# Loads and transforms dealt out as single operations, and in another order, between the steps of two matmul layers

## The chip, the cores and the metric

One Trainium2 chip, one of its cores. Device time in microseconds of one execution; several runs of each kernel, of which the median is given. TensorE, VectorE (DVE), ScalarE (ACT), GpSimd (POOL) and SyncE (SP) each work through a queue of their own, in order, and wait for each other by semaphores.

## What is computed

A two-dimensional Fourier transform of eight sequences of 3008 x 256, of which the real part goes through an MLP with 2048 hidden units.

```python
batch, seq, dim = (8, 3008, 256)
X = np.fft.fft(x, axis=1)
X = np.fft.fft(X, axis=2)
x = X.real.astype(np.float32).reshape(batch * seq, dim)
h = x @ w_in                       # 256 x 2048
r = np.maximum(h, 0.0)
g = s * (r * r) + b
out = (g @ w_out).astype(np.float32)   # 2048 x 256
```

## The kernel before

The transform along the features is folded into `w_in` at the start, and the symmetry of the real transform leaves 1506 columns of each sequence to be computed, each with two outputs ("pm" 0 and 1). The columns of a sequence are cut into three blocks of about 500 (some of 512), and each block goes through 16 steps, one for each 128 hidden units: 8 x 3 x 16 = 384 steps. Precision is kept by splitting each operand into a high part and a low rest and multiplying three times (high by high, low by high, high by low).

A step has these parts. The **first layer** (letter `L`, `first_layer`, L856): six matmuls of 500 columns into one of two pairs of PSUM banks, `ab`. Then the step's **group** on VectorE: L859, L860, L861 read `ab` and write `h`; with the third the banks are free for the first layer two steps later. ScalarE does L874, L875 (relu and square) and L876 (the high part `gh`), and GpSimd L880 the low part `gl` = `h` - `gh`. `h`, `gh` and `gl` have three buffers each. The **second layer** of a step (letter `S`, L897): twelve matmuls on `gh` and `gl` of a step two to four back, summed over the 16 steps of a block in four PSUM banks `po`; after the last, VectorE's L917 (four times) brings the sums out.

Between the steps the next sequences are prepared. `load` takes a sequence in eight tiles of 384 KB; for each a **front part** of three VectorE operations on the tile `xt` (L584, L585, L586), and a **back part** of two (L588, L589) that write `cs`, behind which the fetch of the tile two further on is issued on SP's queue (L575). `transform` (twice a sequence, `ph` 0 and 1) makes inputs (L433, L434, L442 to L446, L424), multiplies them by tables on TensorE (L684, into an `ab` bank pair that it holds until its sums are read), adds the results (L689, L690, L695) and stores them as the first layer's operands: high parts on ScalarE (L667), low ones on GpSimd (L670).

The order of all this is written out by hand. The string `START` deals out the first 57 steps, and `BATCH` is then gone through once for each 48 steps, a **round**: six full rounds with preparation, at about 293 to 1470 us, and one of 39 steps without. In `BATCH` the letter `L` means first layer, group, high and low part of one step, `S` the second layer of the oldest step that has none yet, `l` the next piece of `load`, `v` and `o` the next piece of the two transforms. A piece is what a generator does up to its next `yield`: before, a whole front part, a whole back part, all sums of one transform stage, and so on. At the end `_in_order` ties every engine's instructions to the order in which they were written. Steps are counted here from 1 to 48 within a round, so the 16 steps of a block end with steps 7, 23 and 39.

Of the kernel before, what the change touches and what calls it, by code (L numbers as in the profile page):

```python
# [67 lines left out]
BATCH = (  # L68
# [3 lines left out]
)  # L72
# [218 lines left out]
def kernel(ctx: ExitStack, tc: tile.TileContext, xq, xn, dft, turn, feat, w_in, w_out, s, b, out):  # L291
# [128 lines left out]
    def stt(dst, a, col, other, engine=nc.vector):  # L420
# [4 lines left out]
        else:  # L425
            engine.tensor_mul(dst, a, factor.broadcast_to(dst.shape))
            engine.tensor_add(dst, dst, other)

    def leaves_x(ph, cs, lf, engine=nc.vector):

        a, b_ = cs[:, 2], cs[:, 3]
        if ph == 0:
            engine.tensor_add(lf[:, 0], a, b_)  # L433
            engine.tensor_sub(lf[:, 1], a, b_)  # L434
        else:
            stt(lf[:, 0], b_, 0, a, engine)
            stt(lf[:, 1], a, 4, b_, engine)

    def leaves_y(ph, cs, uv, lf, engine=nc.vector):

        if ph == 0:
            engine.tensor_add(uv[:, :2], cs[:, 4:6], cs[:, 6:])  # L442
            engine.tensor_sub(uv[:, 2:], cs[:, 4:6], cs[:, 6:])
            yield
            engine.tensor_add(lf[:, 0], uv[:, 0], uv[:, 1])
            engine.tensor_sub(lf[:, 1], uv[:, 0], uv[:, 1])  # L446
            stt(lf[:, 2], uv[:, 3], 0, uv[:, 2], engine)
            stt(lf[:, 3], uv[:, 2], 4, uv[:, 3], engine)
        else:
            stt(uv[:, 0], cs[:, 6], 1, cs[:, 4], engine)  # L450
            stt(uv[:, 1], cs[:, 4], 5, cs[:, 6], engine)
            stt(uv[:, 2], cs[:, 7], 2, cs[:, 5], engine)
            stt(uv[:, 3], cs[:, 5], 6, cs[:, 7], engine)
            yield
            stt(lf[:, 0], uv[:, 2], 3, uv[:, 0], engine)
            stt(lf[:, 1], uv[:, 3], 7, uv[:, 1], engine)
            stt(lf[:, 2], uv[:, 2], 7, uv[:, 0], engine)
            stt(lf[:, 3], uv[:, 3], 3, uv[:, 1], engine)
        yield
# [8 lines left out]
    def nyquist(ph, t, room):  # L468
# [109 lines left out]
    def load(su):  # L578

        cs = fold.tile([P, 2, 8, 2 * P], F32, name="cs")  # L580
        folded[su] = cs
        for c in range(8):
            t = fetched.pop(0)
            add(t[:, 0::2], t[:, 0::2], t[:, 1::2])  # L584
            add(t[:, 1], t[:, 0], t[:, 2])  # L585
            sub(t[:, 3], t[:, 0], t[:, 2])  # L586
            yield
            add(cs[:R, :, c, :P], t[:, 1::2, :P], t[:, 1::2, P:])  # L588
            sub(cs[:R, :, c, P:], t[:, 1::2, :P], t[:, 1::2, P:])  # L589
            if 8 * su + c + 2 < 8 * NB:  # L590
                fetch(8 * su + c + 2)
            yield
# [79 lines left out]
    def transform(su, ph):  # L672
# [27 lines left out]

        lf = fold.tile([R, 4, 2 * P], F32, name="lf")
        leaves_x(ph, cs, lf[:, 2:])
        yield
        held, t, l = yield from pair(0, [cs[:, i] for i in range(2)])
        x0 = t[:, :, 2 * NL:].rearrange("p k (r a g) -> p k r a g", r=4, a=2)
        both(x0[:, :, :, 0], x0[:, :, :, 1], *map(by_residue, two(t, l)))
        banks.give(held)
# [3 lines left out]
        if ph == 0:  # L711
            x1 = l.rearrange("p k i (r g) -> p k (i r) g", r=2)
        else:
            x1 = t[:, :, 2 * NL:]
            both(x1[:, :, :NL], x1[:, :, NL:], *two(t, l))
            x1 = by_residue(x1)
        both(x[:, :, :, :2 * G], x[:, :, :, 2 * G:], x0, x1)
        banks.give(held)
# [3 lines left out]
        uv = small.tile([R, 4, 2 * P], F32, name="uv", tag="tmp")  # L722
        y_inputs = leaves_y(ph, cs, uv, lf)
        next(y_inputs)
        yield
        next(y_inputs)
        yield
        for i in range(2):
            held, t, l = yield from pair(4 + 2 * i, [lf[:, 2 * i + n] for n in range(2)])
            if ph == 0 and i == 0:  # L730
                y, which = l, slice(0, 2)
            else:
                y = t[:, :, 2 * NL:].rearrange("p k (r g) -> p k r g", r=2)
                both(y[:, :, 0], y[:, :, 1], *two(t, l))
                which = slice(i, 4, 2) if ph else slice(2, 4)
            o = fold.tile([P, 2, 2, 2, NL], F32, name="o")
            both(o[:, :, :, 0], o[:, :, :, 1], x[:, :, which], y)
            banks.give(held)
            o = o.rearrange("p k r a g -> p k r (a g)")
# [259 lines left out]

    def first():  # L1000
# [6 lines left out]
        steps.append(((su, blk, j), first_layer(su, blk, j, ebc[n])))  # L1007
# [44 lines left out]
    su = 1  # L1052
    while step < NB * NBLOCKS * NJ:
# [48 lines left out]
```

## Time and profile before

| | |
|---|---|
| median of 3 runs | 1677.92 us (1677.06 to 1678.57) |
| the profiled execution | 1679.25 us |
| its span, first to last instruction | 1677.3 us |
| granted TensorE clock, mean over the span | 0.999 |
| busy: PE, DVE, ACT, POOL | 1645.9, 1334.0, 1242.9, 975.6 us |
| bytes moved, mean rate | 67.44 MB, 40 GB/s |

The rows further down come from that one execution. A row of a timeline has the start in us from the span's start, the length in us, engine, line, operation, output<-input, shape, and in brackets the idle time of that engine just ahead of it and what ended it. A matmul's printed length is a model and longer than the distance to the next one. In a list of waits the three numbers are us in total, times, and the longest.

### The profile page before, as it was taken

The numbers are of one execution on the slowest core, as the hardware profiler recorded it, in microseconds if no ns is written. First come the engines' busy times: TensorE is split into PE (matmuls) and PEld (weight loads), VectorE is DVE, ScalarE is ACT, GpSimd is POOL, SyncE is SP. The second block draws the span as 40 slices with busy tenths as digits, with TensorE's granted clock in tenths as the row PEclk, the third lists the DMA queues.
The fourth block names the chain that finished last, engine by engine and source line by source line (L and its number), as shares of the span: only waits on it lengthen the run. The fifth ranks groups of instructions, "written<-read, shape, count | busy, mean of one in ns | idle before, by whom it ended". The sixth has DMA issues, their size and how long they took to land.

```text
span 1677.3 us, 21438 instructions
## 1 busy us (share of the span) xinstructions
PE 1645.9 (98%) x7592; PEld 1374.0 (82%) x7592; DVE 1334.0 (80%) x2010; ACT 1242.9 (74%) x1308; POOL 975.6 (58%) x542
## 2 busy tenths in 40 slices
PE   8999999999999999999999999999999999999998
PEld 5788788788887888878888788887888888888887
DVE  7999989996779867798677976879767896775554
ACT  4986666677686777867777777767878678787776
POOL 5664344555575556655656566555666556666565
PEclk9999999999999999999999999999999999999999
DMA  8211201120012100121100201102001110000100
GB/s 233 77 38 50 69 20 31 38 70 31 1 32 72 35 31 1 41 63 35 32 27 15 72 26 31 31 26 73 18 23 32 38 50 32 1 32 8 24 25 25
DMA packets 34320, 67.44 MB, mean 40 GB/s; under 512 B 7683, under 2 KB 24899, under 8 KB 34214
## 3 DMA queue, kind: packets, MB, share of 16 engines
q1 hardware_dynamic: 34214, 66.09, 13.2%
q8 instruction: 59, 0.97, 0.2%
q14 instruction: 47, 0.39, 0.1%
HBM read 41.35 MB, written 24.73 MB: 39 GB/s over the span
## 4 chain that ended last, share of the span: by engine, by line
PE 79%; DVE 14%; issue 3%; DMA 2%; ACT 1%; POOL 0%; POOLq 0%; SPq 0%; DVEq 0%; ACTq 0%
PE po L897 50%; PE ab L856 25%; PE ab L684 3%; DVE h L859 3%; DVE h L860 3%; DVE xt L584 2%; DVE h L861 2%; DVE xt L586 1%; DVE cs L589 1%; DVE cs L588 1%; DMA raw<-in_w_in 1%; DMA xt<-in_xq 1%; DVE xt L585 0%; ACT h L875 0%; ACT h L874 0%
## 5 line engine op out<-in xcount | busy, mean ns | idle before, releaser
L880 POOL TENSOR_TENSOR gl<-h,gh 128x1000 fp32r<-128x1000 f32 (+2 forms) x365 | 867.9, 2378 | 636.7 <-ACT gh L876 514.2
L874 ACT ACTIVATE h<-h 128x1000 f32<-128x1000 f32 (+2 forms) x380 | 395.3, 1040 | 351.2 <-DVE h L861 347.6
L859 DVE SCALAR_TENSOR_TENSOR h<-ebc,wny,ab 128x500 f32<-128x500 f32 (+1 forms) x384 | 280.8, 731 | 269.5 <-PE ab L856 150.5
L897 PE MATMUL po<-gh,wo_h 128*128 128x500 f32 (+2 forms) x1536 | 470.2, 387 | 0.0
L897 PE MATMUL po<-gl,wo_h 128*128 128x500 f32 (+2 forms) x1536 | 466.6, 385 | 0.8 <-POOL gl L880 0.8
L897 PE MATMUL po<-gh,wo_l 128*128 128x500 f32 (+2 forms) x1536 | 466.2, 385 | 0.0
L876 ACT CAST gh<-h 128x1000 fp32r<-128x1000 f32 (+2 forms) x385 | 397.4, 1032 | 35.2 <-PE po L897 15.8
L875 ACT ACTIVATE h<-h 128x1000 f32<-128x1000 f32 (+2 forms) x380 | 396.2, 1043 | 12.1
L897 PEld LDWEIGHTS po<-gl,wo_h 128*128 128x128 f32 x1536 | 288.1, 188 | 55.8 <-POOL gl L880 3.5
L897 PEld LDWEIGHTS po<-gh,wo_l 128*128 128x128 f32 x1536 | 288.6, 188 | 52.7
L897 PEld LDWEIGHTS po<-gh,wo_h 128*128 128x128 f32 x1536 | 285.8, 188 | 50.8
L856 PE MATMUL ab<-spec_h,wd_h 128*128 128x500 f32 (+1 forms) x768 | 301.5, 393 | 21.9 <-DVE h L861 21.0
L856 PE MATMUL ab<-spec_l,wd_h 128*128 128x500 f32 (+1 forms) x768 | 295.5, 385 | 0.2 <-DVE spec_l L670 0.2
L856 PE MATMUL ab<-spec_h,wd_l 128*128 128x500 f32 (+1 forms) x768 | 295.3, 385 | 0.0
L860 DVE TENSOR_TENSOR h<-h,ab 128x500 f32<-128x500 f32 (+1 forms) x384 | 260.0, 677 | 13.2
L861 DVE TENSOR_TENSOR h<-h,ab 128x500 f32<-128x500 f32 (+1 forms) x384 | 259.9, 677 | 13.2
L856 PEld LDWEIGHTS ab<-spec_h,wd_h 128*128 128x128 f32 x768 | 144.2, 188 | 62.0 <-DVE h L861 34.9
L856 PEld LDWEIGHTS ab<-spec_h,wd_l 128*128 128x128 f32 x768 | 144.3, 188 | 26.6
L856 PEld LDWEIGHTS ab<-spec_l,wd_h 128*128 128x128 f32 x768 | 144.4, 188 | 24.4 <-DVE spec_l L670 0.5
L917 DVE TENSOR_SCALAR o<-po,sb_s,bias 128x500 f32<-128x500 f32 (+1 forms) x94 | 68.8, 795 | 8.7 <-PE po L897 8.6
L584 DVE TENSOR_TENSOR xt<-xt 96x512 f32<-96x512 f32 x56 | 73.7, 1315 | 0.0
L670 POOL TENSOR_TENSOR spec_l<-o,spec_h 128x368 fp32r<-128x368 f32 (+7 forms) x75 | 60.0, 813 | 18.9 <-ACT spec_h L667 17.7
(128 smaller groups left out, 775.4 us busy)
## 6 DMA issues: line engine op xcount, KB each, us to landing
xt<-in_xq SPq DMA_DIRECT2D x64, 384.0 KB
out<-o SPq DMA_DIRECT2D x38, 500.0 KB
raw<-in_w_in SPq DMA_DIRECT2D x8, 512.0 KB
raw<-in_w_out SPq DMA_DIRECT2D x8, 512.0 KB
out<-o SPq DMA_DIRECT2D x8, 506.0 KB
ebc<-e_dram SPq DMA_DIRECT2D x12, 250.0 KB
ebc<-e_dram SPq DMA_DIRECT2D x4, 253.0 KB
out<-o SPq DMA_DIRECT2D x4, 250.0 KB
```

The costliest lines, as they stand in the source:

```text
L584: add(t[:, 0::2], t[:, 0::2], t[:, 1::2])
L670: low_engine.tensor_sub(lo, src, hi.bitcast(F32))
L856: nc.tensor.matmul(ps[:, kind], w[:, kind, fj], m[:, kind], start=i == 0, stop=i == 2)
L859: nc.vector.scalar_tensor_tensor(h[:, 0], ebc, wny[:, j:j + 1], ps[:, 0], op0=ALU.mult, op1=ALU.add)
L860: sub(h[:, 1], h[:, 0], ps[:, 1])
L861: add(h[:, 0], h[:, 0], ps[:, 1])
L874: nc.scalar.activation(h[:, pm], h[:, pm], AF.Relu)
L875: nc.scalar.activation(h[:, pm], h[:, pm], AF.Square)
L876: nc.scalar.copy(gh[:, pm, :width], h[:, pm])
L880: engine.tensor_sub(gl[:, pm, :width], h[:, pm], gh[:, pm, :width].bitcast(F32))
L897: nc.tensor.matmul(po[2 * pm + dh][:, :n], l[:, j, dh * P:(dh + 1) * P], r[:, pm, :n], start=start and first, stop=stop and last,)
L917: nc.vector.tensor_scalar(dst, src, *args, ALU.mult, ALU.add)
```

## The change

`load`, `transform` and their helpers yield `MORE` behind every single operation, and a plain `yield` where a piece ended before. `START` takes pieces whole as before, by the new function `whole`. `BATCH` takes one operation for each letter: 40 `l`, 28 `v` and 36 `o` in place of 16, 11 and 11, and its order is new. A step can also be written `H`: its low part on GpSimd is then done in two operations, one for each of the two outputs (`V`, on VectorE, does not occur in the table). `H` stands at steps 16, 39 and 48. Excerpt:

```diff
 BATCH = (
-    "L l S L L S l S L l l S L l l S l L S l L S L S l L l L S S L L S l l S L l S S L L l L l S L v l S L S S L L S "
+    "L l S l l L L l l S S l l l L l l l S l l L l l S l l l L S l l L S L S l L l l L S l l S L L S l l "
+    "l l l S L l l l S S L l l L l l l S H v v l S L S l S L L S L v S v v v L v v v v v S L v v v v L S "
...
+    def whole(pieces):
+
+        for more in pieces:
+            if more is not MORE:
+                return
...
     def load(su):
...
             add(t[:, 0::2], t[:, 0::2], t[:, 1::2])
+            yield MORE
             add(t[:, 1], t[:, 0], t[:, 2])
+            yield MORE
             sub(t[:, 3], t[:, 0], t[:, 2])
             yield
             add(cs[:R, :, c, :P], t[:, 1::2, :P], t[:, 1::2, P:])
+            yield MORE
             sub(cs[:R, :, c, P:], t[:, 1::2, :P], t[:, 1::2, P:])
...
         def both(dst_a, dst_b, a, b_):
             add(dst_a, a, b_)
+            yield MORE
             sub(dst_b, a, b_)
...
-    def first_layer(su, blk, j, ebc):
+    def first_layer(su, blk, j, ebc, low):
...
-        engine = nc.vector if step in LOWS_OF_STEPS_ON_VECTOR else nc.gpsimd
-        for pm in rows:
+        engine = nc.vector if step in LOWS_OF_STEPS_ON_VECTOR or low == "V" else nc.gpsimd
+        for pm in rows if low != "H" else (0, 1):
             engine.tensor_sub(gl[:, pm, :width], h[:, pm], gh[:, pm, :width].bitcast(F32))
...
+        elif what in "uvol":
+            whole(work[what])
...
         for what in BATCH.split():
-            if what == "L" and step < NB * NBLOCKS * NJ:
-                first()
-                go_on_first()
-                next(lows.pop(0))
+            if what in "LHV":
+                if step < NB * NBLOCKS * NJ:
+                    first(what)
+                    go_on_first()
+                    next(lows.pop(0))
```

What it moves: of the load, the front part of the second tile from step 4 to behind the back part at step 3, and of the third and fourth tile likewise by one place; the fifth tile's front part is cut, L584 at step 8 and the other two at step 9, and its back part stands at step 10; the last L589 goes from step 16 to step 17. One L424 of the second transform goes from step 37 to 36. A second layer goes ahead of the first layer of step 24, and one ahead of that of step 44. All else on TensorE, VectorE and ScalarE stands as before; the lines after L32 carry other numbers (L584 to L589 are L597 to L605, L859 to L861 are L880 to L882, L880 is L901).

VectorE's queue in the second round, from the back part of step 3 on, before (`xt` with a number is one tile, `h` with a number one step):

```order
L588 TENSOR_TENSOR cs_4174<-xt_2996 96x2x128
L589 TENSOR_TENSOR cs_4174<-xt_2996 96x2x128
L859 SCALAR_TENSOR_TENSOR h_4259<-ebc_3580,wny_94,ab_4252 128x500
L860 TENSOR_TENSOR h_4259<-h_4259,ab_4252 128x500
L861 TENSOR_TENSOR h_4259<-h_4259,ab_4252 128x500
L584 TENSOR_TENSOR xt_3055<-xt_3055 96x2x256
L585 TENSOR_TENSOR xt_3055<-xt_3055 96x256
L586 TENSOR_TENSOR xt_3055<-xt_3055 96x256
L588 TENSOR_TENSOR cs_4174<-xt_3055 96x2x128
L589 TENSOR_TENSOR cs_4174<-xt_3055 96x2x128
L859 SCALAR_TENSOR_TENSOR h_4295<-ebc_3580,wny_94,ab_4288 128x500
```

and now:

```order
L603 TENSOR_TENSOR cs_4177<-xt_2996 96x2x128
L605 TENSOR_TENSOR cs_4177<-xt_2996 96x2x128
L597 TENSOR_TENSOR xt_3097<-xt_3097 96x2x256
L599 TENSOR_TENSOR xt_3097<-xt_3097 96x256
L601 TENSOR_TENSOR xt_3097<-xt_3097 96x256
L880 SCALAR_TENSOR_TENSOR h_4265<-ebc_3581,wny_94,ab_4258 128x500
L881 TENSOR_TENSOR h_4265<-h_4265,ab_4258 128x500
L882 TENSOR_TENSOR h_4265<-h_4265,ab_4258 128x500
L603 TENSOR_TENSOR cs_4177<-xt_3097 96x2x128
L605 TENSOR_TENSOR cs_4177<-xt_3097 96x2x128
L597 TENSOR_TENSOR xt_4229<-xt_4229 96x2x256
L599 TENSOR_TENSOR xt_4229<-xt_4229 96x256
```

The front part of the second tile stands ahead of step 4's group, and every pile between two groups of steps 3 to 6 has a back and a front part; before, the pile behind step 5 had eight operations.

VectorE's queue around steps 8 to 10 of the same round, from the end of step 8's group, before:

```order
L861 TENSOR_TENSOR h_4396<-h_4396,ab_4389 128x500
L584 TENSOR_TENSOR xt_4310<-xt_4310 96x2x256
L585 TENSOR_TENSOR xt_4310<-xt_4310 96x256
L586 TENSOR_TENSOR xt_4310<-xt_4310 96x256
L859 SCALAR_TENSOR_TENSOR h_4428<-ebc_4125,wny_94,ab_4421 128x500
L860 TENSOR_TENSOR h_4428<-h_4428,ab_4421 128x500
L861 TENSOR_TENSOR h_4428<-h_4428,ab_4421 128x500
L588 TENSOR_TENSOR cs_4174<-xt_4310 96x2x128
L589 TENSOR_TENSOR cs_4174<-xt_4310 96x2x128
L859 SCALAR_TENSOR_TENSOR h_4449<-ebc_4125,wny_94,ab_4442 128x500
L860 TENSOR_TENSOR h_4449<-h_4449,ab_4442 128x500
L861 TENSOR_TENSOR h_4449<-h_4449,ab_4442 128x500
```

and now:

```order
L882 TENSOR_TENSOR h_4399<-h_4399,ab_4392 128x500
L597 TENSOR_TENSOR xt_4313<-xt_4313 96x2x256
L880 SCALAR_TENSOR_TENSOR h_4429<-ebc_4127,wny_94,ab_4422 128x500
L881 TENSOR_TENSOR h_4429<-h_4429,ab_4422 128x500
L882 TENSOR_TENSOR h_4429<-h_4429,ab_4422 128x500
L599 TENSOR_TENSOR xt_4313<-xt_4313 96x256
L601 TENSOR_TENSOR xt_4313<-xt_4313 96x256
L880 SCALAR_TENSOR_TENSOR h_4448<-ebc_4127,wny_94,ab_4441 128x500
L881 TENSOR_TENSOR h_4448<-h_4448,ab_4441 128x500
L882 TENSOR_TENSOR h_4448<-h_4448,ab_4441 128x500
L603 TENSOR_TENSOR cs_4177<-xt_4313 96x2x128
L605 TENSOR_TENSOR cs_4177<-xt_4313 96x2x128
```

The front part is in two, and the back part stands behind step 10's group, ahead of the four L917 (now L938) of the block that ended with step 7.

GpSimd's queue from the end of the first round's stores through the second round's low parts (`gl`), before:

```order
L670 TENSOR_TENSOR spec_l<-o,spec_h 128x2x184
L670 TENSOR_TENSOR spec_l<-o,spec_h 128x2x186
L880 TENSOR_TENSOR gl<-h,gh 128x2x500 x30
L670 TENSOR_TENSOR spec_l<-o,spec_h 128x2x190
L670 TENSOR_TENSOR spec_l<-o,spec_h 128x2x188
```

and now:

```order
L686 TENSOR_TENSOR spec_l<-o,spec_h 128x2x184
L686 TENSOR_TENSOR spec_l<-o,spec_h 128x2x186
L901 TENSOR_TENSOR gl<-h,gh 128x500 x2
L901 TENSOR_TENSOR gl<-h,gh 128x2x500 x15
L901 TENSOR_TENSOR gl<-h,gh 128x500 x2
L901 TENSOR_TENSOR gl<-h,gh 128x2x500 x13
L686 TENSOR_TENSOR spec_l<-o,spec_h 128x2x190
```

The first pair of halves belongs to step 48 of the first round, the second to step 16 of the second; with the last step of all there are 20 such pairs.

## Rows read from the trace of the kernel before

**Rows 1.** The page, part 1: busy us and share, instructions.

```profile
PE 1645.9 (98%) x7592; PEld 1374.0 (82%) x7592; DVE 1334.0 (80%) x2010; ACT 1242.9 (74%) x1308; POOL 975.6 (58%) x542
```

**Rows 2.** Waits of TensorE, its weight loads, 290 to 1470; 495 to 545.

```profile
PE ab L856 <- DVE h L861: 14.5, 15, 1.4
...
PEld ab L856 <- DVE h L861: 25.4, 30, 1.8
...
PE ab L856 <- DVE h L861: 2.7, 3, 1.4
```

**Rows 3.** Timeline of TensorE, second round, steps 7, 8 and 12.

```profile
519.14 0.49 PE L856 MATMUL ab<-spec_h,wd_h 128*128 128x500 f32 x1 [0.18 <-DVE h L861]
...
522.77 0.60 PE L897 MATMUL po<-gl,wo_h 128*128 128x500 f32 x2
524.78 0.49 PE L856 MATMUL ab<-spec_h,wd_h 128*128 128x500 f32 x1 [1.41 <-DVE h L861]
525.11 0.38 PE L856 MATMUL ab<-spec_l,wd_h 128*128 128x500 f32 x1
525.33 0.38 PE L856 MATMUL ab<-spec_h,wd_l 128*128 128x500 f32 x1
...
539.37 0.50 PE L856 MATMUL ab<-spec_h,wd_h 128*128 128x500 f32 x1 [1.12 <-DVE h L861]
```

**Rows 4.** Timeline of VectorE, second round, steps 3 to 6.

```profile
506.31 0.42 DVE L589 TENSOR_TENSOR cs<-xt 96x256 f32<-96x256 f32 x1
508.51 0.73 DVE L859 SCALAR_TENSOR_TENSOR h<-ebc,wny,ab 128x500 f32<-128x500 f32 x1 [1.78 <-PE ab L856]
...
510.58 2.80 DVE L584 TENSOR_TENSOR xt<-xt 96x512 f32<-96x512 f32 x1
...
514.20 2.48 DVE L588 TENSOR_TENSOR cs<-xt 96x256 f32<-96x256 f32 x1
...
519.00 0.68 DVE L584 TENSOR_TENSOR xt<-xt 96x512 f32<-96x512 f32 x1
...
522.58 0.72 DVE L859 SCALAR_TENSOR_TENSOR h<-ebc,wny,ab 128x500 f32<-128x500 f32 x1
...
524.05 0.68 DVE L861 TENSOR_TENSOR h<-h,ab 128x500 f32<-128x500 f32 x1
```

**Rows 5.** The same view, steps 8 to 10.

```profile
531.41 2.58 DVE L586 TENSOR_TENSOR xt<-xt 96x256 f32<-96x256 f32 x1
...
535.98 0.94 DVE L588 TENSOR_TENSOR cs<-xt 96x256 f32<-96x256 f32 x1
...
538.64 0.68 DVE L861 TENSOR_TENSOR h<-h,ab 128x500 f32<-128x500 f32 x1
```

**Rows 6.** Timeline of GpSimd, low parts of steps 2, 3, 4, 7.

```profile
507.40 2.36 POOL L880 TENSOR_TENSOR gl<-h,gh 128x1000 fp32r<-128x1000 f32 x1 [2.85 <-ACT gh L876]
510.48 2.36 POOL L880 TENSOR_TENSOR gl<-h,gh 128x1000 fp32r<-128x1000 f32 x1 [0.72 <-ACT gh L876]
514.06 2.34 POOL L880 TENSOR_TENSOR gl<-h,gh 128x1000 fp32r<-128x1000 f32 x1 [1.23 <-ACT gh L876]
...
531.21 2.50 POOL L880 TENSOR_TENSOR gl<-h,gh 128x1000 fp32r<-128x1000 f32 x1 [0.72 <-ACT gh L876]
```

**Rows 7.** Timeline of ScalarE, step 4: first and last operation.

```profile
510.75 1.04 ACT L874 ACTIVATE h<-h 128x1000 f32<-128x1000 f32 x1 [0.41 <-DVE h L861]
...
512.90 1.03 ACT L876 CAST gh<-h 128x1000 fp32r<-128x1000 f32 x1
```

**Rows 8.** Groups by line and shape: busy us, mean ns, idle before.

```profile
L880 POOL TENSOR_TENSOR gl<-h,gh 128x1000 fp32r<-128x1000 f32 x302 | 715.6, 2370 | 536.8 <-ACT gh L876 442.2 <-DVE h L860 16.5 <-PE ab L856 15.3
...
L880 POOL TENSOR_TENSOR gl<-h,gh 128x500 fp32r<-128x500 f32 x2 | 2.8, 1424 | 1.1 <-ACT gh L876 1.1
```

**Rows 9.** Timeline, second layer of the last step.

```profile
1669.91 0.38 PE L897 MATMUL po<-gh,wo_l 128*128 128x500 f32 x1
...
1670.84 0.50 PE L897 MATMUL po<-gl,wo_h 128*128 128x500 f32 x1 [0.55 <-POOL gl L880]
```

More of the change, by code (lines that the diff above doesn't have):

```diff
@@ L31 @@
 NJ = FF // P
+MORE = "more"
 ENGINES = tuple(getattr(mybir.EngineType, e) for e in ("PE", "DVE", "Activation", "Pool", "SP"))
@@ L436, in leaves_x @@
             stt(lf[:, 0], b_, 0, a, engine)
+            yield MORE
             stt(lf[:, 1], a, 4, b_, engine)
+        yield
     def leaves_y(ph, cs, uv, lf, engine=nc.vector):
@@ L445, in leaves_y @@
             engine.tensor_add(lf[:, 0], uv[:, 0], uv[:, 1])
+            yield MORE
             engine.tensor_sub(lf[:, 1], uv[:, 0], uv[:, 1])
+            yield MORE
             stt(lf[:, 2], uv[:, 3], 0, uv[:, 2], engine)
+            yield MORE
             stt(lf[:, 3], uv[:, 2], 4, uv[:, 3], engine)
         else:
[L450 to L458, printed above, removed]
+            for k, (a, col, b_) in enumerate(((6, 1, 4), (4, 5, 6), (7, 2, 5), (5, 6, 7))):
+                stt(uv[:, k], cs[:, a], col, cs[:, b_], engine)
+                yield MORE if k < 3 else None
+            for k, (a, col, b_) in enumerate(((2, 3, 0), (3, 7, 1), (2, 7, 0), (3, 3, 1))):
+                stt(lf[:, k], uv[:, a], col, uv[:, b_], engine)
+                yield MORE if k < 3 else None
+            return
         yield
@@ L477, in nyquist @@
         nc.gpsimd.tensor_copy(lf[:, :2], cs[:, :2])
-        leaves_x(ph, cs, lf[:, 2:4], nc.gpsimd)
+        whole(leaves_x(ph, cs, lf[:, 2:4], nc.gpsimd))
         for _ in leaves_y(ph, cs, uv[:, :4], lf[:, 4:], nc.gpsimd):
@@ L584, in load @@
             add(t[:, 0::2], t[:, 0::2], t[:, 1::2])
+            yield MORE
             add(t[:, 1], t[:, 0], t[:, 2])
+            yield MORE
             sub(t[:, 3], t[:, 0], t[:, 2])
@@ L588, in load @@
             add(cs[:R, :, c, :P], t[:, 1::2, :P], t[:, 1::2, P:])
+            yield MORE
             sub(cs[:R, :, c, P:], t[:, 1::2, :P], t[:, 1::2, P:])
@@ L689, in both @@
             add(dst_a, a, b_)
+            yield MORE
             sub(dst_b, a, b_)
@@ L701, in transform @@
         lf = fold.tile([R, 4, 2 * P], F32, name="lf")
-        leaves_x(ph, cs, lf[:, 2:])
-        yield
+        yield from leaves_x(ph, cs, lf[:, 2:])
         held, t, l = yield from pair(0, [cs[:, i] for i in range(2)])
         x0 = t[:, :, 2 * NL:].rearrange("p k (r a g) -> p k r a g", r=4, a=2)
-        both(x0[:, :, :, 0], x0[:, :, :, 1], *map(by_residue, two(t, l)))
+        a, b_ = map(by_residue, two(t, l))
+        yield MORE
+        yield from both(x0[:, :, :, 0], x0[:, :, :, 1], a, b_)
         banks.give(held)
@@ L714, in transform @@
             x1 = t[:, :, 2 * NL:]
-            both(x1[:, :, :NL], x1[:, :, NL:], *two(t, l))
+            a, b_ = two(t, l)
+            yield MORE
+            yield from both(x1[:, :, :NL], x1[:, :, NL:], a, b_)
+            yield MORE
             x1 = by_residue(x1)
-        both(x[:, :, :, :2 * G], x[:, :, :, 2 * G:], x0, x1)
+        yield from both(x[:, :, :, :2 * G], x[:, :, :, 2 * G:], x0, x1)
         banks.give(held)
@@ L722, in transform @@
         uv = small.tile([R, 4, 2 * P], F32, name="uv", tag="tmp")
[L723 to L727, printed above, removed]
+        yield from leaves_y(ph, cs, uv, lf)
         for i in range(2):
@@ L733, in transform @@
                 y = t[:, :, 2 * NL:].rearrange("p k (r g) -> p k r g", r=2)
-                both(y[:, :, 0], y[:, :, 1], *two(t, l))
+                a, b_ = two(t, l)
+                yield MORE
+                yield from both(y[:, :, 0], y[:, :, 1], a, b_)
+                yield MORE
                 which = slice(i, 4, 2) if ph else slice(2, 4)
             o = fold.tile([P, 2, 2, 2, NL], F32, name="o")
-            both(o[:, :, :, 0], o[:, :, :, 1], x[:, :, which], y)
+            yield from both(o[:, :, :, 0], o[:, :, :, 1], x[:, :, which], y)
             banks.give(held)
+            yield MORE
             o = o.rearrange("p k r a g -> p k r (a g)")
             for _ in store(su, ph, [(r, o[:, :, m]) for m, r in enumerate(range(4)[which])]):
-                pass
+                yield MORE
             yield
@@ L998, in load_e, with first @@
                     )
-    def first():
+    def first(low=None):
         nonlocal step
@@ L1006, in first @@
             load_e(n + 1)
-        steps.append(((su, blk, j), first_layer(su, blk, j, ebc[n])))
+        steps.append(((su, blk, j), first_layer(su, blk, j, ebc[n], low)))
         next(steps[-1][1])
```

5 rows, old and new, of the table BATCH are left out of this document.

## The prediction

> **What bounds the kernel now.** I read the page's first part first: TensorE is busy for 98% of the span, VectorE for 80%, ScalarE 74%, GpSimd 58% [rows 1]. TensorE is the bound, so a gain is only what TensorE idles, or what makes it late. The list of waits, cut to the six rounds (290 to 1470 us), says where that is: the first layer's matmul waits for VectorE's L861 15 times, for 14.5 us (three of them in the second round, 495 to 545); its weight loads name the same releaser 30 times [rows 2]. The rounds repeat one table, so the second stands for all.
>
> The timeline of TensorE shows what a wait costs. Undisturbed, one 500-column matmul starts every 0.22 us (525.11, 525.33), though its bar is 0.38 long; so a printed idle of 1.41 before 524.78 is 1.41 + 0.16 = 1.57 us lost, and the matmul behind it starts 0.33 later instead of 0.22, 0.11 more [rows 3]. All 15 waits: 14.5 + 15 x (0.16 + 0.11) = 18.6 us. In the second round they stand before steps 7 (519.14), 8 (524.78) and 12 (539.37) [rows 3]: a step k needs one of the two "ab" banks, and step k-2's VectorE group (L859 to L861) must have left it. That group is late since VectorE's queue holds the load's pieces ahead of it. From 508.51, where the group of step 4 still waited 1.78 us for TensorE, VectorE has no idle row until step 10's group ends at 538.64 + 0.68 = 539.3 [rows 4, 5].
>
> What fills that stretch is partly waiting inside the bars. L584 takes 0.68 at 519.00, but 2.80 at 510.58, 0.10 us after GpSimd began a 2.36 us low subtraction; L588 takes 2.48 at 514.20 in the same way, against 0.42 for its twin L589 at 506.31. Each ends 0.3 to 0.5 us after GpSimd's does [rows 4, 6]. At 531.21 it goes finely: GpSimd's operation comes while VectorE is between single operations, is let in (2.50 instead of 2.36), and L586, 0.20 later, takes 2.58 [rows 5, 6]. So a piece costs its own time plus whatever is left of a GpSimd subtraction that is running.
>
> **The change, part by part.** (1) *Single operations.* Nothing is added: the transforms' operations keep their places between the steps (one of the L424 group moves behind a second layer, still ahead of step 37's group); only the load's move. (2) *Steps 3 to 8.* The front part (L584 to L586) that made step 5's pile eight operations long goes ahead to step 3; steps 3, 4 and 5 now have five each. I work the second round through with the durations of rows 4 to 7. A group takes 2.1 us (508.51 to 510.58); a back and a front part without a collision 2.2; GpSimd's subtraction comes 3.4 us after a group's end (group end 510.66, ScalarE from 510.75 to 512.90 + 1.03, GpSimd at 514.06) and lasts 2.36 [rows 6, 7].
> Step 3's back part ends at 506.73. The front part behind it fills the 1.78 us in which VectorE idled, but GpSimd arrives at 507.40, in its middle. As at 531, I let it in, and L586 waits: 507.40 + 0.15 + 2.36 + 0.28 = 510.2. Step 4's group: 510.2 to 512.3, 1.7 later than before. Its five operations meet GpSimd's 510.48 to 512.84 only at its end (L588 done 513.1) and are through at 514.85, before GpSimd's next at 512.3 + 3.4 = 515.7. Step 5's group: to 516.95, where before it ended with the L584 of 519.00. Next five: L588 waits until 518.1, the rest ends at 520.1; step 6's group to 522.2 (before: 524.73). TensorE wants step 7 at 519.14 - (0.18 + 0.16) = 518.8 and step 8 18 matmuls later, at 522.76: both groups are there, with 1.85 and 0.55 to spare.
> (3) *Steps 8 to 10.* A front part is cut (L584 at step 8, L585 and L586 at step 9) and its back part goes behind step 10's group. On from 522.2: back part to 523.35 (GpSimd until 522.7), groups 7 and 8 to 527.5, L584 to 528.55 (GpSimd 525.6 to 528.0), group 9 to 530.65, L585 and L586 to 531.85 (GpSimd until 531.2, ScalarE pacing it 3.2 us behind the last), group 10 to 533.95. Step 12 is due 60 matmuls after step 8, at 535.96: 2.0 to spare. So the three waits should go: up to 18.6 us in six rounds. What is late next is step 8 with its 0.55.
> (4) *If the tie at 507.40 falls the other way*, the front part is through before GpSimd and step 4's group stays at 508.51. Then its pile runs into two subtractions (512.84 and one from 514.15 to 516.5) and group 5 ends at 519.25: step 7 is 0.45 + 0.11 late, step 8 another 0.25 + 0.11, about 0.9 a round or 5.4 us. I charge a third of that, 1.8 us, as the 531 pattern is the nearer row.
> (5) *Halves.* 20 low subtractions (steps 16, 39, 48) are two operations. A whole one takes 2.37 us on average, a half 1.42 in the two cases that there are [rows 8]: at most 0.48 us more each, 9.6 us on GpSimd, which idles for 42% of the span; TensorE names it as releaser nowhere in the three places above, so zero on the path. If that cover were gone it would be up to 9.6. It also lets a VectorE operation in half way, which I count as zero in steps 16 and 39.
> [...]
> (6) *The last step* is such a half. At the end TensorE stops for 0.55 + 0.16 us (1670.84) plus 0.11, for the low part of the last step [rows 9]. Half of it comes about 0.95 us earlier (2.37 - 1.42): 0.8 gained.
> (7) *A second layer ahead of steps 24 and 44.* It reads results that are two or three steps old; the 15 waits of rows 2 all stand elsewhere, and a first layer that comes 12 x 0.22 = 2.6 us later has the other bank as cover. Zero; at most 0.5 x 6 = 3 us if step 45's bank, which a transform pair holds, is late.
> (8) *DMA.* The next tile's fetch goes out with each L589, on SP's queue, which holds the outputs too; those come behind the same VectorE operations as before. The shortest distance from a fetch to its use was about 4.2 us: from the L589 behind 514.20 + 2.48, at about 517.0, to the last three of the eight operations from 519.00 to 522.58, at about 521.2, and they ran without a wait [rows 4]. Now it is about 5.3 (513.45 to 518.7). Zero.
>
> The sum: 18.6 + 0.8 - 1.8 = 17.6 us. The profiled execution took 1679.25 with a span of 1677.3; the median of the runs is 1677.92. All of the gain lies inside the span, so I take it off the median: about 1660.
>
> **The rivals.** *The wait shrinks but stays.* The sum rests on which of two engines comes first within 0.1 us. For: at 507.40 and 514.15 it is a tie. If all rounds go by (4), the loss is 5.4 instead of 1.8: 1664. If step 12's wait stays too (1.12 + 0.27 a round, 8.3 in all), 1672. Against: 0.65 us or more to spare at step 12 even then.
> *Nothing changes.* VectorE's queue has no idle between steps 4 and 10; the same operations in another order take as long, unless collisions get fewer. The waiting inside the bars of that stretch was at least 6.9 us (2.12, 2.07, 2.17 and 0.53 in [rows 4, 5]) and is 5.0 by (2) and (3) (2.2, 0.4, 1.1, 0.45, 0.4 and 0.45); the idle 1.78 is used up, and 0.75 us (the back part) leaves the stretch. If the collisions grow by as much as the idle and the back part give, only the last step's 0.8 is left: 1677.
> *Slower: each piece meets a subtraction of its own.* Cutting a front part and putting one into a gap makes two more places where VectorE turns from its groups to these operations in a round. Where each pays in full what L586 paid at 531 (2.58 - 0.41 = 2.2 us), step 10's group comes 4.4 later, less the 1.78 + 0.75: about 1.9 a round on the path, 11 us: 1689. It decides from the point where step 10's group ends more than 32.6 us after step 3's back part (506.73 to 539.3 before). For: operations in one pile pay once or not at all, as from 519.00 to 522.58, where eight ran without a wait. Against: in (3) the cut parts meet only the last 0.5 us of a subtraction.
>
> **How the numbers follow.** The forecast, 1655 to 1663: 0.60. The wait stays in part, 1664 to 1674: 0.20. Nothing changes: 0.08. Slower: 0.12. The low end: all 15 waits gone (18.6), the last step (0.8), and the other 15 late weight loads at most 0.27 each (4): 1677.9 - 23.4 = 1654.5. The high end takes in the first rival: 1673. A measurement of this kernel can tell about 0.2% (3.4 us) from no change. Faster by more: 0.60 + 0.20 and a little of the third, 0.82; within: 0.07; slower: 0.11.
>
> **What would show it.** In the changed kernel's list of waits, "PE ab <- DVE h" in the six rounds should fall from 14.5 us to under 3. The timeline should show step 4's group at about 1.7 us later than before and the groups of steps 5 and 6 about 2 us earlier against TensorE's pace; L586 of step 3 with a bar of over 2 us is the tie falling as I took it. Step 10's group should end before step 11's matmuls do. The last low part should no longer hold TensorE. I am wrong if bars of L584 to L589 above 2 us are more, not fewer, between steps 3 and 10, or if a new wait for GpSimd's low parts appears before the second layer.

## The result, and the profile after

The changed kernel takes 1654.9 us in the median of four runs (1653.2 to 1656.5), the kernel before 1677.9 beside it: a ratio of 0.986, 95% interval 0.985 to 0.988, or 23.0 us. Run again, it gave 1653.5 (0.984 to 0.987). The forecast was 1660; the result lies at the fast end of it, 0.1 us below the 1655 to 1663 that had the chance of 0.60, and 0.4 above the low end of 1654.5.

The page of the changed kernel: busy time of the engines [rows 1], and the chain of work that ended last, by engine.

```profile
PE 1639.5 (99%) x7592; PEld 1379.0 (83%) x7592; DVE 1322.7 (80%) x2010; ACT 1242.6 (75%) x1308; POOL 982.6 (59%) x562
...
PE 95%; DVE 3%; issue 1%; DMA 0%; SPq 0%; ACT 0%; DVEq 0%
```

The share of the span says little; the stretch of the rounds says more. Busy time from 300 to 1460 us (start:end, length, then PE, weight loads, DVE, ACT, POOL, TensorE's granted clock, DMA share, GB/s), first of the kernel before:

```profile
300.00:1460.00 1160.00, 1145.13 (x5313) 965.87 (x5312) 940.26 (x1400) 866.99 (x884) 695.13 (x333) 1.00 0.12 35
```

and of the changed one:

```profile
300.00:1460.00 1160.00, 1160.00 (x5417) 988.31 (x5416) 946.65 (x1428) 886.60 (x903) 715.33 (x356) 1.00 0.12 35
```

TensorE has no idle left in the rounds. The list of waits agrees: the 15 waits and 30 late weight loads of [rows 2] have no row any more between 290 and 1450 us, neither "PE" nor "PEld" stands on its left side. VectorE's longest wait there is the one for TensorE, up from 94.2 us, 61 times:

```profile
DVE h L880 <- PE ab L877: 99.2, 70, 2.1
```

Now the place itself, second round, steps 3 to 6, 8 to 10 (VectorE), which answers to [rows 4, 5]. L597 to L601 are the front part, L603 and L605 the back part, L880 to L882 a group.

```profile
504.43 0.41 DVE L605 TENSOR_TENSOR cs<-xt 96x256 f32<-96x256 f32 x1
...
505.83 2.58 DVE L601 TENSOR_TENSOR xt<-xt 96x256 f32<-96x256 f32 x1
508.34 0.72 DVE L880 SCALAR_TENSOR_TENSOR h<-ebc,wny,ab 128x500 f32<-128x500 f32 x1
...
518.17 0.72 DVE L880 SCALAR_TENSOR_TENSOR h<-ebc,wny,ab 128x500 f32<-128x500 f32 x1
...
528.61 0.92 DVE L599 TENSOR_TENSOR xt<-xt 96x256 f32<-96x256 f32 x1
...
531.26 0.68 DVE L882 TENSOR_TENSOR h<-h,ab 128x500 f32<-128x500 f32 x1
```

GpSimd and TensorE beside it, [rows 6] and [rows 3]:

```profile
505.52 2.62 POOL L901 TENSOR_TENSOR gl<-h,gh 128x1000 fp32r<-128x1000 f32 x1 [3.13 <-DVE xt L597]
...
533.80 0.38 PE L877 MATMUL ab<-spec_h,wd_h 128*128 128x500 f32 x1
```

The one bar above 2 us of the load's operations in steps 3 to 10 is L601 of step 3, where there were three (in each of the six rounds; in the first it is L599, with 2.65). Step 10's group ends at 531.94, and step 12's first layer starts at 533.80 without a wait.

For the experiments I added up, from each timeline of TensorE, by how much every start came later than the regular 0.22 us after the one before it (0.11 for a transform's 96 columns), over the six rounds. It includes the slower second matmul behind a wait (its start comes 0.33 us after the first's in place of 0.22 [rows 3]). A loss of about 0.1 us around each pair of a transform's matmuls is in all kernels and left out. "Behind 17 to 19" is lost at two places: within the second layer of step 15, where TensorE waits for that step's low part (1.7 us in the kernel before), and ahead of the first layer of step 19, which waits for VectorE (1.6).

| lost by TensorE, us, six rounds | time | ratio | before steps 7, 8 | before 10 | before 12 | behind 17 to 19 | pair behind 20 | last step |
|---|---|---|---|---|---|---|---|---|
| before | 1677.9 | 1 | 12.0 | 0 | 7.6 | 3.4 | 0 | 0.8 |
| after | 1654.9 | 0.986 | 0 | 0 | 0 | 0 | 0 | 0 |
| first half only | 1663.1 | 0.991 | 0 | 0 | 4.9 | 3.3 | 0 | 0.8 |
| second half only | 1670.8 | 0.995 | 12.0 | 0 | 0 | 0 | 3.0 | 0.8 |
| whole lows | 1658.0 | 0.987 | 0 | 0 | 0 | 0 | 2.8 | 0.8 |
| halves only | 1677.7 | 0.999 | 11.7 | 0 | 7.8 | 3.2 | 0 | 0 |
| second layers back | 1654.3 | 0.985 | 0 | 0 | 0 | 0 | 0 | 0 |
| uncut front part | 1660.2 | 0.990 | 0 | 0 | 2.7 | 2.2 | 0 | 0 |
| spread evenly | 1676.3 | 0.998 | 0 | 12.4 | 2.3 | 6.0 | 0 | 0.8 |
| zeros for low parts | 1655.1 | 0.986 | 0 | 0 | 0 | 0 | 0 | 0.8 |
| halves where held | 1676.9 | 0.999 | 9.5 | 0 | 8.2 | 3.0 | 0 | 0.8 |

Times are medians; the ratio is to runs of the kernel before on the same chip (1678.4 to 1679.0 for all but the second line), with intervals of 0.001 to 0.002 to either side. In "uncut front part" nearly all of the 2.7 stand in the second layer that follows step 12's first layer, not ahead of that first layer.

### The profile page after: what moved, and what is told of

Same layout as the page of the kernel before. It is cut to its first block, busy times and chain, and to the rows that moved or that the text cites. A ratio compares the mean times of both kernels' runs of the same rounds, so it can differ in the third digit from the quotient of the medians.

```text
span 1654.8 us, 21458 instructions
## 1 busy us (share of the span) xinstructions
PE 1639.5 (99%) x7592; PEld 1379.0 (83%) x7592; DVE 1322.7 (80%) x2010; ACT 1242.6 (75%) x1308; POOL 982.6 (59%) x562
## 4 chain that ended last, share of the span: by engine, by line
PE 95%; DVE 3%; issue 1%; DMA 0%; SPq 0%; ACT 0%; DVEq 0%
PE po L918 60%; PE ab L877 30%; PE ab L700 3%; PE ab L393 1%; DVE h L880 1%; DVE h L881 1%; DVE h L882 1%; PE po L815 1%; DMA unit<-in_turn 0%; DVE uv L426 0%; PE po L621 0%; PE po L618 0%; PE ab L542 0%; DVE wd_l L320 0%; DVE h L893 0%
## 5 line engine op out<-in xcount | busy, mean ns | idle before, releaser
L901 POOL TENSOR_TENSOR gl<-h,gh 128x1000 fp32r<-128x1000 f32 (+3 forms) x385 | 875.6, 2276 | 606.3 <-ACT gh L897 440.9
L880 DVE SCALAR_TENSOR_TENSOR h<-ebc,wny,ab 128x500 f32<-128x500 f32 (+1 forms) x384 | 280.6, 731 | 258.7 <-PE ab L877 149.8
L877 PE MATMUL ab<-spec_h,wd_h 128*128 128x500 f32 (+1 forms) x768 | 297.7, 388 | 7.3 <-DVE h L882 7.0
L882 DVE TENSOR_TENSOR h<-h,ab 128x500 f32<-128x500 f32 (+1 forms) x384 | 259.9, 677 | 13.2
L938 DVE TENSOR_SCALAR o<-po,sb_s,bias 128x500 f32<-128x500 f32 (+1 forms) x94 | 68.7, 791 | 8.0 <-PE po L918 7.9
L603 DVE TENSOR_TENSOR cs<-xt 96x256 f32<-96x256 f32 x56 | 58.5, 1045 | 0.3
```

Of the source, the lines that this page charges most:

```text
L877: nc.tensor.matmul(ps[:, kind], w[:, kind, fj], m[:, kind], start=i == 0, stop=i == 2)
L880: nc.vector.scalar_tensor_tensor(h[:, 0], ebc, wny[:, j:j + 1], ps[:, 0], op0=ALU.mult, op1=ALU.add)
L882: add(h[:, 0], h[:, 0], ps[:, 1])
L938: nc.vector.tensor_scalar(dst, src, *args, ALU.mult, ALU.add)
```

## The experiments

**The two halves of the reordering.** In both kernels the low subtractions are whole and everything else stands as before, in single operations. In the first, steps 1 to 5 are the changed ones:

```diff
-3 L S l l S       4 L l l l l l S   5 L l l l l l S l l l
+3 L l l S S l l l 4 L l l l S l l   5 L l l S l l l
```

> Only the first half of the reordering: steps 1 to 7 of each round as in the changed kernel (the front part moved to step 3, five load operations each in steps 3, 4 and 5), the rest of the round in the old order, no halves. My theory (the pile of step 5 is what makes VectorE late, and all that follows inherits it): the waits before steps 7, 8 and 12 all go, since step 10's group, with its uncut front part and the back part ahead of it (0.8 us more than in the changed kernel, where it ends at 531.93 in the second round), still ends before step 12 is due at about 535: 18.6 us, about 1659. What the changed kernel gained beyond that (23.0 - 18.6 = 4.4 us) stays away, since steps 16 to 19 and the last step are as before. Rival (step 12's wait is freed by the cut in steps 8 to 10): only the 11 us of steps 7 and 8 go, about 1667. Rival (slower, a collision at 507.40 for nothing): 1678 or more.

Measured: 1663.1 us, ratio 0.991 (0.989 to 0.992), 15.9 us. Steps 7 and 8 are free, but step 12 keeps most of its loss. The rows show what I had left out. Timeline of all engines, second round, steps 8 to 12:

```profile
524.22 2.44 POOL L901 TENSOR_TENSOR gl<-h,gh 128x1000 fp32r<-128x1000 f32 x1 [0.79 <-ACT gh L897]
...
524.36 2.58 DVE L601 TENSOR_TENSOR xt<-xt 96x256 f32<-96x256 f32 x1
...
532.39 0.50 PE L877 MATMUL ab<-spec_h,wd_h 128*128 128x500 f32 x1 [0.80 <-DVE h L882]
```

I had counted 0.8 us for the back part. But the uncut front part also runs into the next subtraction, which its third operation pays with 2.58 us. So the place is decided by the cut as well.

In the second kernel only steps 8 to 17 are the changed ones:

```diff
-8 L S l l l  10 L S S      16 L v v l l S  17 L S S
+8 L S l      10 L S l l S  16 L v v l S    17 L S l S
```

> Only the second half of the reordering: steps 8 to 17 as in the changed kernel (front part cut between steps 8 and 9, back part behind step 10's group, the last back part cut between 16 and 17), steps 1 to 7 in the old order, no halves. My theory: the waits before steps 7 and 8 stay (11 us), step 12's 1.12 + 0.27 us shrinks by the back part that leaves the stretch (0.8 us) to about 0.5: gain 4 to 6 us; and the small lateness in steps 17 to 19 (3 us in six rounds) goes if the cut at step 16 is its cause: together 1669 to 1674. Rival (the second half does the work): 1660 or less. Rival (a cut part pays a second collision): 1678 to 1684.

Measured: 1670.8 us, ratio 0.995 (0.993 to 0.996), 8.2 us. Step 12's wait goes altogether, where I had left it 0.5, and so does the lateness behind steps 17 to 19; but 3.0 us come in new, at the transform pair behind step 20:

```profile
PE ab L877 <- DVE h L882: 8.6, 9, 1.4
...
PE ab L700 <- DVE h L882: 1.8, 4, 0.5
```

Alone the two halves give 15.9 + 8.2 = 24.1 us. Both together, with whole low subtractions, give 21.0 (1658.0, the run "whole lows" below): they overlap at step 12, whose loss the second half takes away altogether and the first by 2.7 us. That 24.1 is near the 23.0 of the whole change is chance, since the change has the halved subtractions besides.

**One cut alone.** The changed kernel, with the front part of steps 8 and 9 in one piece:

```diff
-8 L S l      9 L l l
+8 L S l l l  9 L
```

> The changed kernel with one thing undone: the front part of steps 8 and 9 in one piece at step 8; its back part stays behind step 10's group. Theory (in the run with the first half only, L601 of the uncut part waited 2.58 us for a subtraction that the cut avoids): L601 waits about 2.4 us again, the group of step 9 comes 2.4 to 3 us later, step 10's group ends at about 533.7 in the second round where step 12 starts at 533.80: no wait or up to 0.3 us a round, 1655 to 1657. Rival (the cut is needed, as the back part is): about 0.8 us a round as in that run, 1660.

Measured: 1660.2 us, ratio 0.990 (0.988 to 0.991); my range was too low, and the time is the rival's. L601 waits as in the run above; step 10's group ends at 532.19 and step 12's first layer comes just in time at 532.29. But then the output copies (L938) behind that group are late, and TensorE's second layer needs their banks. VectorE, and TensorE's weight load:

```profile
525.48 2.58 DVE L601 TENSOR_TENSOR xt<-xt 96x256 f32<-96x256 f32 x1
...
531.51 0.68 DVE L882 TENSOR_TENSOR h<-h,ab 128x500 f32<-128x500 f32 x1
532.78 0.79 DVE L938 TENSOR_SCALAR o<-po,sb_s,bias 128x500 f32<-128x500 f32 x1
...
534.33 0.19 PEld L918 LDWEIGHTS po<-gh,wo_h 128*128 128x128 f32 x1 [0.46 <-DVE o L938]
```

I had followed one reader of VectorE's queue, the "ab" banks, and not the next one.

**The halves.** The changed kernel with its 20 halved low subtractions whole (`H` as `L`):

> The changed kernel with the 20 halved low subtractions whole again. My theory (halves are worth the last step's 0.8 us and nothing else): 1655.7, the 0.55 us wait before the last matmuls back, and no other wait. Rival (the halves at steps 16 also freed steps 17 to 19, where 15 late weight loads stood): up to 3.4 us more, about 1659, with the weight loads naming GpSimd's gl again. [...]

Measured: 1658.0 us, ratio 0.987 (0.986 to 0.989), 3.1 and 4.6 us above the changed kernel's medians of 1654.9 and 1653.5 (2.0 and 4.1 when each is taken against the kernel before beside it, and the intervals overlap). TensorE's losses make it 3.6: 0.8 at the last step, and 2.8 where my theory had nothing, at the pair behind step 20, as in the run with the second half. The cause, as far as the rows show it, stands at step 17, where the load's last L605 now is. With a whole subtraction (timeline of all engines):

```profile
560.84 2.36 POOL L901 TENSOR_TENSOR gl<-h,gh 128x1000 fp32r<-128x1000 f32 x1 [2.81 <-ACT gh L897]
...
560.96 2.52 DVE L605 TENSOR_TENSOR cs<-xt 96x256 f32<-96x256 f32 x1
...
567.66 1.13 PE L700 MATMUL ab<-dft_sb,cs 96*128 96x96 f32 x8 [0.46 <-DVE h L882]
```

and in the changed kernel, with halves:

```profile
563.31 2.69 POOL L901 TENSOR_TENSOR gl<-h,gh 128x500 fp32r<-128x500 f32 x2 [2.82 <-ACT gh L897]
...
563.43 1.44 DVE L605 TENSOR_TENSOR cs<-xt 96x256 f32<-96x256 f32 x1
...
569.44 1.03 PE L700 MATMUL ab<-dft_sb,cs 96*128 96x96 f32 x8
```

L605 is let in between the halves, 1.08 us earlier, and the pair doesn't wait. So the half at step 16 pays for the operation that the same change put at step 17. The kernel before with the halves and nothing else:

> The kernel before with nothing but the 20 halved low subtractions. My theory: 0.8 us at the last step, 1677.1. Rival (the half at step 16 frees steps 17 to 19): 1674. Rival (two operations cost GpSimd 0.36 us more each and let VectorE and GpSimd meet once more): up to 7 us slower, 1685.

Measured: 1677.7 us, ratio 0.999 (0.998 to 1.000); the last step's 0.8, and the lateness behind 17 to 19 stays. Would more halves do in place of another order? The old order, with the low subtractions of steps 2 to 10 halved:

> The kernel before, in its old order, with the low subtractions of steps 2 to 10 of each round halved (54 of them). Theory, from the run without halves (with the half, L605 of step 16 was let in after 1.44 us, without it after 2.52): a half holds a load operation for 1.4 us instead of 2.5, so three long bars a round give back about 1 us each, VectorE's group of step 6 comes 2 us earlier and the waits before steps 7 and 8 go, step 12's at least in part: 11 to 18 us, 1660 to 1667. Rival (an operation that gets in between the halves only makes the next one meet the second half): no change, 1678. Rival (0.36 us more on GpSimd per step makes the low parts late for the second layer): slower, up to 54 x 0.36 = 19 us.

Measured: 1676.9 us, ratio 0.999 (0.998 to 1.000): nearly nothing, the first rival. The pile of five behind step 4, VectorE and GpSimd:

```profile
510.10 2.96 POOL L901 TENSOR_TENSOR gl<-h,gh 128x500 fp32r<-128x500 f32 x2 [0.56 <-POOL gl L901]
...
510.21 1.72 DVE L597 TENSOR_TENSOR xt<-xt 96x512 f32<-96x512 f32 x1
...
511.96 1.38 DVE L599 TENSOR_TENSOR xt<-xt 96x256 f32<-96x256 f32 x1
...
513.27 0.41 DVE L601 TENSOR_TENSOR xt<-xt 96x256 f32<-96x256 f32 x1
...
513.70 2.68 POOL L901 TENSOR_TENSOR gl<-h,gh 128x500 fp32r<-128x500 f32 x2 [0.63 <-POOL gl L901]
...
513.71 1.53 DVE L603 TENSOR_TENSOR cs<-xt 96x256 f32<-96x256 f32 x1
...
515.17 1.49 DVE L605 TENSOR_TENSOR cs<-xt 96x256 f32<-96x256 f32 x1
```

Four operations wait a half each, where two waited for a whole one. A half helped a single operation (L605 of step 17, 1.44 us for 2.52), with the group behind it; in this pile the next operation met the other half.

**What holds the load's operations.** The kernel before in its old order; in steps 2 to 10 GpSimd writes zeros and subtracts nothing:

```diff
+            if step >= 57 and 2 <= (step - 57) % 48 + 1 <= 10:
+                nc.gpsimd.memset(gl[:, pm, :width].bitcast(F32), 0.0)
+            else:
                 engine.tensor_sub(gl[:, pm, :width], h[:, pm], gh[:, pm, :width].bitcast(F32))
```

> The kernel before, but in steps 2 to 10 of each round GpSimd fills gl with zeros (it only writes) instead of subtracting: the low parts of these steps are left out, everything else, and the order, is as before. Theory (a load operation of VectorE with two operands in memory waits while GpSimd's subtraction runs): the bars of L584 to L589 in steps 3 to 9 fall to 0.68 and 0.42, none above 1.1 us, the 6.9 us of waiting inside bars go, and with them all 15 waits of TensorE: 18.6 us, 1659. Rival (the pile itself, 8 operations ahead of a group, is what makes it late): at least the waits before steps 7 and 8 stay, 1667 to 1672. Rival (the long bars come from something else, a transfer or ScalarE): bars and time as before, 1678.

Measured: 1655.1 us, ratio 0.986 (0.984 to 0.987), as fast as the changed kernel without its last-step half. The order is the old one, with eight operations in step 5's pile, so it isn't the pile by itself. GpSimd's operation is shorter here, too (0.93 us for 2.36); that it isn't the length alone is shown by a row in which the two run side by side. The same operations on VectorE, with GpSimd's writing among them:

```profile
504.92 0.68 DVE L584 TENSOR_TENSOR xt<-xt 96x512 f32<-96x512 f32 x1
...
505.50 0.93 POOL L881 MEMSET gl<- 128x1000 f32 x1 [3.02 <-PE po L900]
...
505.63 0.42 DVE L585 TENSOR_TENSOR xt<-xt 96x256 f32<-96x256 f32 x1
```

L585 runs in its 0.42 while GpSimd writes. With a subtraction in its place it is otherwise: of the kernel before, all 66 of the load's operations that begin while a subtraction runs, in the six rounds, end 0.28 to 0.29 us behind it, L584 0.54 to 0.55. L584, begun 0.10 us after a subtraction, took 2.80 us [rows 4, 6], against 0.68 here. The group's operations, which read `ab` (L860 and L861 with `h`), keep their time: those that begin while a subtraction runs take 0.67 to 0.69 us (L860, L861) and 0.72 to 0.75 (L859), as they do without one. Whether GpSimd's reading or something else of the subtraction is what counts, no run tells.

**The even spread.** The load's 40 operations as three and two in turn behind steps 1 to 16:

> The load's 40 operations of a round dealt out evenly: three and two in turn behind each of the steps 1 to 16, the rest in the old order, no halves. Rival of the prediction (each piece meets a low subtraction of its own): 16 places instead of 11 where VectorE turns from a group to these operations, each with up to 2.2 us of waiting inside a bar; the waits before steps 7, 8 and 12 stay and others come: 1678 to 1700. My theory after the first runs (what counts is whether GpSimd starts while such an operation is next, place by place, and how much slack the next group has): some collisions more, some less; the pile of step 5 is gone, so steps 7 and 8 gain 11 us, and step 12 keeps its wait, as with the uncut front part: 1665 to 1675. Third theory (an even spread is simply best): below 1655.

Measured: 1676.3 us, ratio 0.998 (0.998 to 0.999). Steps 7 and 8 are free; step 10 waits instead, for 12.4 us (1.6 of them late starts of the matmuls behind one of the waits). The front parts of steps 3, 5, 7 and 9 on VectorE, and TensorE at step 10, second round:

```profile
505.71 2.46 DVE L599 TENSOR_TENSOR xt<-xt 96x256 f32<-96x256 f32 x1
...
514.15 2.47 DVE L599 TENSOR_TENSOR xt<-xt 96x256 f32<-96x256 f32 x1
...
522.72 2.47 DVE L599 TENSOR_TENSOR xt<-xt 96x256 f32<-96x256 f32 x1
...
527.64 0.49 PE L877 MATMUL ab<-spec_h,wd_h 128*128 128x500 f32 x1 [1.58 <-DVE h L882]
...
531.12 2.51 DVE L599 TENSOR_TENSOR xt<-xt 96x256 f32<-96x256 f32 x1
```

Each front part meets a subtraction of its own, with 2.05 us (2.47 - 0.42): the prediction's slower rival, close to the 2.2 that it gave. But the old waits of steps 7 and 8 are gone with step 5's pile, and the sum is a kernel no slower than before. My own theory (step 12 keeps its wait, 1665 to 1675) missed, too: the time lies 1.3 us above its range, step 12 keeps 2.3 of its 7.6 us, and it didn't see the wait at step 10.

**The second layers ahead of steps 24 and 44**, back in their old places in the changed kernel:

```diff
-23 L S S  24 L S    43 L S o o o o o o o o S  44 L
+23 L S    24 L S S  43 L S o o o o o o o o    44 L S
```

> The changed kernel with the two second layers ahead of steps 24 and 44 back in their old places. Theory (they read results that are two or three steps old, and no wait stood there): the same time, 1653.5 to 1655; the 0.12 us that TensorE loses before each transform pair only moves from step 43 back to step 44. Rival (they took part in the gain): up to 3 us back, 1657.

Measured: 1654.3 us, ratio 0.985 (0.983 to 0.987), beside 1653.5 and 1654.9. No part of the gain; the 0.1 us around a pair moves from step 43 to step 44, as expected.

**A faster one, by the same reasoning.** What is left to TensorE's waits stands in `START`, which the change doesn't touch: in the changed kernel 0.60 and 0.47 us at 165.18 and 167.25, 1.84 at 177.31, 1.60 at 277.05, each for VectorE's L882. I moved pieces that stand ahead of the awaited groups behind them.

```diff
-L L S l L L S D D D S l G l G L L D l D l S     ... S o o L o S S L L D D o S S D
+L L S L L S D D l D S l G G L L D l l D l S     ... S o o L S S L L D o D o S S D
```

> The changed kernel with three pieces moved in the opening part, by the same reasoning: two back parts of the load go behind the VectorE groups that TensorE waits for (the waits of 0.60, 0.47 and 1.84 us at 165.18, 167.25 and 177.31 in the changed kernel), and four operations of L426 go behind the group at 274.82 (1.60 us at 277.05). Theory: all four waits go, 5.2 us with their start-to-start losses, and the half-speed matmuls that follow the 1.84 us wait (8 x 0.195 = 1.6 us) may go with it: 1648 to 1650 where the changed kernel has 1655. Rival (the moved pieces meet GpSimd in their new place and the next group is late instead): 1653 to 1656. Rival (L684 or a transform's copy behind the moved L426 operations becomes late): 1656 to 1660.

Measured: 1652.4 us, ratio 0.984 (0.983 to 0.986). Three waits are gone, and that of 1.84 us has grown to 2.56, as the front part ahead of its group is now held. VectorE, TensorE:

```profile
168.99 2.49 DVE L597 TENSOR_TENSOR xt<-xt 96x512 f32<-96x512 f32 x1
...
174.38 0.49 PE L877 MATMUL ab<-spec_h,wd_h 128*128 128x500 f32 x1 [2.56 <-DVE h L882]
```

So I put that piece behind the group, too, beside the changed kernel itself once more.

```diff
-S D D l D S l G G L L D l l D l S
+S D D l D S G G L L D l l D l l S
```

> The start of the kernel with moved pieces again, with one place mended: in the run before, the first three waits went, but the fourth grew to 2.56 us, since the front part of the load stood ahead of the group at 172.19 and its L597 waited 2.49 us for GpSimd. Here that front part goes behind this group as well. Theory: the group ends at about 171.2 where TensorE wants it at 171.8, the wait goes with the half-speed matmuls behind it (2.7 + 8 x 0.195 = 4.3 us): 1648. Rival (the five operations now between the two groups make the next group late): 1650 to 1653. Rival (the half-speed stretch has another cause than the wait): 1650.

> The changed kernel itself, on the chip of these runs, to compare the others with: 1655 to 1656.5.

Measured: 1653.3 us, ratio 0.985 (0.984 to 0.987), and the changed kernel 1653.5. The wait at 174.38 is gone, and two groups later there is a longer one, behind the next front part:

```profile
181.94 2.45 DVE L599 TENSOR_TENSOR xt<-xt 96x256 f32<-96x256 f32 x1
...
187.63 0.79 PE L877 MATMUL ab<-spec_h,wd_h 128*128 128x500 f32 x1 [3.73 <-DVE h L882]
```

Neither is faster than the changed kernel by more than its own medians differ (1653.5, 1654.9), and the theory that the waits of the start would simply go has fallen: in that stretch VectorE has hardly a gap (busy for 6.86 of the 7.00 us from 168 to 175 in the changed kernel), and a moved piece moves the wait. A version that clearly beats the changed kernel was not found.

## Why the prediction was right, and where its sum was off

**Waits of steps 7, 8 and 12, 18.6 us: right, in mechanism and size.** TensorE's losses there fall from 19.6 us to nothing (most of the difference to 18.6 is three late starts before step 7, 0.9 in all, which no row lists as a wait). That the subtraction holds the load's operations, and with them the group, is shown by the run with zeros. Even the moments came out. Counted from the end of step 3's back part (504.84 after), the prediction had step 4's group at +3.47, step 6's at +13.37 and the end of step 10's at +27.2; they came at +3.50, +13.33 and +27.10. Step 12 was to have 2.0 us to spare and had 1.86.

**The tie, a charge of 1.8: not due.** L601 of step 3 took 2.58 us with GpSimd let in ahead of it, just as assumed from the row at 531 [rows 5, 6] (in the first round L599 paid, with 2.65), and no round lost anything. Since the charge was a third of a case that didn't come, this is 1.8 of the 5.4 us by which the sum's 17.6 fell short of 23.0 (with the 3.4 below and the 1.0 above it would be 6.2; single runs of one kernel lie that little apart).

**The other 15 late weight loads, zero: mis-sized; what stood behind steps 17 to 19 cost 3.4 us.** I had kept them for the low end only. Six of the 15, ahead of step 19's first layer, make 1.6 of the 3.4. The other 1.7 are a wait that the prediction didn't list: TensorE's second layer of step 15 waits for GpSimd's low part once a round. The kernel before, 290 to 1470 us:

```profile
PEld po L897 <- POOL gl L880: 2.5, 6, 0.7
```

(Of the 15, three more are the late starts before step 7, and six stand before step 40, for 0.3 us in all.) In the eleven kernels of the table the loss behind 17 to 19 is there exactly where step 12 loses something, whatever stands at steps 12 to 17: it is there with the uncut front part, where those steps are the changed ones, and gone with the zeros, where they are the old ones. So VectorE carries its lateness on from step 12. In the kernel before its queue has no idle row from 508.51 to 570.21, the end of step 17's group, which step 19 waits for; in the changed kernel it waits 0.58 us for TensorE already ahead of step 14's group (548.59). No run changes this stretch alone.

**Halves in steps 16 and 39: not zero.** The one at step 16 saves 2.8 us; without it the operation moved to step 17 would have cost them. That the sum didn't suffer is luck, as the two cancel: I had listed neither the cost nor the gain. GpSimd is busy for 59% of the span, and its halves cost 1.35 us each where I had 1.42 (the page of the changed kernel, by shape):

```profile
L901 POOL TENSOR_TENSOR gl<-h,gh 128x500 fp32r<-128x500 f32 x36 | 47.8, 1346 | 29.7 <-ACT gh L897 15.7 <-DVE h L882 9.4 <-issue 4.6
```

**The last step, 0.8: right** (0.8 with and without the other changes). **Second layers moved and DMA, zero: right**, the first by its own run, the second in that no wait for a transfer stands in the list.

**The rivals.** That the wait stays in part would have come with either half of the change alone (1663 and 1671). The slower one is a real mechanism with the price that I gave, as the even spread shows; the change avoids it, by the places of its cuts. Its total of held time tells little: the load's operations take 14 us more than before in the even spread and 10 us less in the changed kernel, while the times are 2.7 and 23.0 us shorter.

## What to carry over

In this kernel an operation of the load on VectorE (0.42 or 0.68 us by itself) that began while a GpSimd subtraction (2.36) ran ended 0.28 or 0.55 us behind it; so lay such operations out against GpSimd's starts, and judge a place by whether the next group is late for TensorE, not by how much waiting there is in all. Follow every reader of the late queue (banks of both layers, low parts, the next transform), since a wait that is taken away in one place can stand up again further on, as at the pair behind step 20 and in both runs on `START`. Halving the GpSimd operation helped where a single operation stood ahead of a group, and not in a pile.

## What I had not expected of the hardware

GpSimd pays too, and by more than the 0.14 us (2.50 for 2.36) that the prediction read from the row at 531. In the changed kernel its subtraction of 505.52 started 0.03 us after L599 (505.49, 0.42 long), the second of a front part's three operations. Its bar is 2.62 us long, against 2.36 to 2.37 in the other steps from 3 to 10, and L601 behind it took 2.58. Not every start within such an operation is like that: at 541.24, 0.05 us before the end of L601, it took 2.37.

A wait of TensorE cost more than its length in some executions and not in others. After 1.84 us of idle (177.31) the matmuls of the profiled changed kernel started every 0.42 us in place of 0.22 for a while: the granted clock was 0.50. In another execution of the same kernel, behind the same wait of 1.84 us (there at 174.90), it stayed at 1.00 (175 to 177 and 178.80 to 182). The same columns as in the second view (the last four are the engine POOL, the granted clock, the DMA share and GB/s), first the one and then the other:

```profile
178.80:182.00 3.20, 3.20 (x9) 2.59 (x8) 3.13 (x6) 0.66 (x1) 0.00 (x0) 0.50 0.00 0
```

```profile
178.80:182.00 3.20, 3.20 (x16) 2.75 (x15) 3.17 (x5) 3.13 (x4) 0.00 (x0) 1.00 0.44 125
```

Nine matmuls instead of sixteen, about 1.6 us of that execution. Twelve of the traced executions have a wait of this length (1.83 to 1.84 us) ahead of the same step of the opening; behind it the matmuls started every 0.41 to 0.42 us in four (the kernel before among them, with a granted clock of 0.50 from 177 to 180) and every 0.22 to 0.23 in eight. Why they slow down in one and not in another stays open.
